# Warm-up products in fp32, and two loads moved behind DMA transposes, in a fused recurrent attention and MLP kernel

## The chip, the cores and the metric

The kernel runs on one core of one Trainium2 chip. The metric is the time of one execution in microseconds on the device. Before the change it is 179.27 us, the median of three runs (178.81, 179.27, 180.53).

In the text, PE is the matrix engine and PEld its loading of weights, DVE the vector engine, ACT the scalar engine, POOL the GpSimd engine, SP the engine that issues every DMA of this kernel. PSUM is the memory that PE writes to.

## What is computed

A linear recurrence with decay (4 sequences, 8 heads, 768 positions, head size 48) feeds a two-layer MLP with squared ReLU (width 384, inner width 2048). Cut to what matters:

```python
for t in range(S):                       # S = 768
    cur = einsum('bhd,bhe->bhde', u * k[t], v[t])
    y[t] = einsum('bhd,bhde->bhe', r[t], state + cur)
    state = w[t][..., None] * state + einsum('bhd,bhe->bhde', k[t], v[t])
x = y.transpose(0, 2, 1, 3).reshape(B * S, H * D)      # 3072 x 384
h = maximum(x @ w_in, 0)                               # 3072 x 2048
out = (h * h) @ w_out                                  # 3072 x 384
```

All inputs and the output are fp32 in HBM.

## The kernel before

The work is cut into 12 steps, each of 256 positions of one sequence (three steps to a sequence); two positions that follow each other share a partition. A step has an attention part and an MLP part, and the MLP of a step runs long after its attention, so that the attention of later steps fills in beside it.

**Attention of step s.** Loads bring r, k, v and w into fp32 tiles (four buffers for each, `load_step`, L179). `ww_`, `rw_` and `kw_` multiply the decays into the pairs of positions, `lw_` takes the logarithm, `cum_` sums the logarithms with triangular matrices on PE (L332 to L336), `exp_` turns the sums into decays (L348), `rd_` multiplies them into r and k (`rdec_buf` L366, `kdec_buf` L369). Both must be transposed. In the first steps PE does that (`tr_`, L382, then a copy out of PSUM, `rkt_`, L396); from step 4 on a DMA transpose does (`dtr_`, L401 for r, L404 for k). Then come the products r k (`p_`, L422 or L425), their mask on DVE (`pm_`, L438 or L441), the state (`su_`, `ts_`, `sn_`), the output (`y_`, L490, and `yc_`, L502), and the diagonal part with u (`ku_`, `qp_`, `q_`, `qs_`, `vq_`), which is added at the end in `ysb_` (L513). `ub_` (L212) spreads u over the partitions at the start with one fp32 product, and `uc_` copies it out of PSUM.

**MLP of step s.** x is transposed, by PE in the first steps (`yt_`, `xt_`), by DMA from step 6 on (`dyt_`, L534). `m1_` (L545) makes one eighth of the inner width, six products of 256 columns each; `rl_` and `sq_` are the squared ReLU; `m2_` (L576) adds four products of 384 columns into an output bank; `os_` scales it and `store` writes it out.

**What sets the order.** The order of all work is written out by hand, as one list of words (`ORDER`). A word such as `m1_.7.4:3` names an operation, its step and part, and after the colon the PSUM bank; `=A`, `=V` or `=G` names ACT, DVE or POOL. Each engine takes its own words strictly in the order of the list, and waits on the others by semaphores; all DMAs, the transposes among them, are issued by SP one after the other, and SP stops at a word whose input or buffer isn't ready. Where two words sit on different engines, their order in the list does not matter beyond that.

**Dummies.** `warm_.n.i.x` (L594) issues n products of a zero tile into bank i (banks 4 and 5 are the attention's, L596 is the line of each product). They compute nothing that is used: they keep PE busy in the first 24 us while it waits for loads and for DVE. The tile `warm` is cleared on DVE first (L234). There are 55 in all, in thirteen words: 11 before the sums of step 0; 8, 3 and 5 around its transposes; 3, 2 and 7 in one row ahead of the transposes of step 1; then 2, 2, 6, 4, 1 and 1.

The lists of SP around the two moved loads are, before the change: `store.4.1`, `ld.9.v`, `ld.10.k`, `dyt_.7`, `ld.10.v`, `store.4.0`, `dtr_.9.0`, `ld.10.r`, `dyt_.8`, `ld.11.w`, `dtr_.9.1`, `ld.11.v`.

Of the kernel before, what the change touches and what calls it, by code (L numbers as in the profile page):

```python
# [8 lines left out]
FP32 = mybir.dt.float32  # L9
FP16 = mybir.dt.float16  # L10
BF16 = mybir.dt.bfloat16
# [3 lines left out]


ORDER = """
ld.0.w ld.0.u ld.0.k ld.0.r ld.1.w ww_.0=V lw_.0 warm_.11.5.0 cum_.0:0 ub_.0:2 kw_.0=G exp_.0 uc_.0=A rd_.0.1 ld.0.v
warm_.8.5.1 tr_.0.1:0 rkt_.0.1=A ld.1.k ld.1.r rw_.0=G ld.2.w ku_.0=G rd_.0.0 ld.1.v warm_.3.5.2 tr_.0.0:1 ww_.1=V
rkt_.0.0=A qp_.0=V ld.2.r v_.0=A warm_.5.5.3 p_.0.0:m p_.0.1:1 ac_.0 lw_.1 q_.0 su_.0:b ld.2.k cum_.1:0 ts_.0.0=A  # L20
kw_.1=G pm_.0.0 pm_.0.1 vs_.0.0=A sn_.0.0 ld.1.i exp_.1 rw_.1=G vs_.0.1=A qs_.0=A warm_.3.2.4 ku_.1=G rd_.1.0 rd_.1.1
warm_.2.2.5 ts_.0.1=V qp_.1=V warm_.7.2.6 ld.0.i tr_.1.0:0 rkt_.1.0=V warm_.2.3.21 tr_.1.1:2 ac_.1 sn_.0.1 q_.1
# [40 lines left out]
p_.8.0:m p_.8.1:0 kw_.9=G qp_.9=G ysb_.7=V cum_.9:1 m2_.6.0.1:1 ld.9.v ld.10.k os_.5.0=A m2_.6.0.3 m2_.6.1.3:0  # L63
m2_.6.0.0 sq_.6.2=V m2_.6.0.2 m2_.6.1.0 sn_.8.0 al_.9 exp_.9 pm_.8.0 rd_.9.0 pm_.8.1 dyt_.7 v_.9=A ac_.9 m1_.7.7:2
y_.8:0 yc_.8.1 rd_.9.1 su_.9:1 vs_.9.1=A yc_.8.0 rl_.7.7=A m1_.7.4:3 ld.10.v vq_.8=G ysb_.8=V m1_.7.0:2 lw_.10
store.4.0 q_.9 rl_.7.4=A ts_.9.0=A rl_.7.0=A cum_.10:0 al_.10 vs_.9.0=V exp_.10 m2_.6.1.1 os_.6.0=V m2_.6.1.2
os_.6.1=A m1_.7.5:2 m1_.7.6:3 m1_.7.2:0 kw_.10=G dtr_.9.0 qs_.9=G rl_.7.5=A ld.10.r dyt_.8 ld.11.w sq_.7.2=A m1_.7.3:2
m1_.7.1:1 rl_.7.6=A dtr_.9.1 m1_.8.5:3 rl_.7.3=A rl_.7.1=A m1_.8.6:2 v_.10=G sn_.9.0 ts_.9.1=V rw_.10=G rd_.10.1
# [24 lines left out]
def kernel(  # L93
# [13 lines left out]
    nc = tc.nc  # L107
# [3 lines left out]
    C = 128  # L111
# [24 lines left out]
    consts = ctx.enter_context(tc.tile_pool(name="consts", bufs=1))  # L136
# [10 lines left out]
    att = [ps_att.tile([C, 2, 512], FP32, name=f"att{i}") for i in range(2)]  # L147
# [4 lines left out]
    quad = bk + m1_bank  # L152
# [63 lines left out]

    warm = consts.tile([C, 512], BF16)
    tri_strict = consts.tile([C, C], BF16)  # L220
    tri_incl_neg = consts.tile([C, C], BF16)
    ident = consts.tile([C, C], BF16)
# [369 lines left out]
        nc.sync.dma_start(out=out[t0:t0 + C, cols], in_=tiles["o", s, rows][:, cols])  # L592

    def warm_(n, i, x=0):  # L594
        for _ in range(n):
            nc.tensor.matmul(quad[i][:] if i < 4 else att[i - 4][:, 0, :], warm[:, 0:C], warm[:],  # L596
                             start=True, stop=True)

    def ld(n, x, h=None):
# [48 lines left out]
```

## Time and profile before

| | us |
|---|---|
| median of three runs | 179.27 |
| the profiled execution | 180.34 |
| its span, first to last instruction | 178.6 |
| PE busy | 172.8 (97%) |
| DVE busy | 138.9 (78%) |
| ACT busy | 134.0 (75%) |
| POOL busy | 109.7 (61%) |

The profile is of one execution. Times in it count from the first instruction. A row of a timeline is the start, the time until the last of the row's instructions ends, the engine, the line of the kernel, the operation, what it writes and reads, the shape, how many instructions the row holds, and in brackets the idle time of the engine before it with what ended it. The ends of PE's products are modelled and products are pipelined, so a row's end overlaps the next row's start. A product of PE appears as a matmul and a weight load (PEld). A few matmuls are missing from the records (51 of the 55 dummies are there). A row of SP shows when a DMA was issued, not when it landed; the median time from issue to landing stands in a table of the page.

### The profile page before, as it was taken

To read this page: it belongs to the slowest core of one execution; us is meant where nothing else is said; L and a number is where in the kernel's file an instruction comes from. 1 tells how busy PE (TensorE), PEld (TensorE's weight loads), DVE (VectorE), ACT (ScalarE), POOL (GpSimd) and SP (SyncE) were. 2 spreads that over 40 slices of the span, in tenths; PEclk is the share of its full clock that TensorE was granted. 3 is DMA by queue.
4 is the path that set the end of the run, shared out by engine and by line. 5 is a ranking of instruction groups with operands and counts; after the bars stand their busy time and mean duration, and the time that the engine had idled before them with its cause. 6 is when DMAs were issued, how large, how long until landed. Compare 5 with 4: busy or idle time off the path is not lost.

```text
span 178.6 us, 5531 instructions
## 1 busy us (share of the span) xinstructions
PE 172.8 (97%) x2296; PEld 125.6 (70%) x2300; DVE 138.9 (78%) x205; ACT 134.0 (75%) x240; POOL 109.7 (61%) x132
## 2 busy tenths in 40 slices
PE   7999999999999999999999999899999999999993
PEld 2365588887766777678677776588676778868763
DVE  5399999779999997998988999876678693803530
ACT  5478999999799759899789979579876528853601
POOL 6458999861765437997599689959997803000000
DMA  5999999999999499999999999998997650512212
GB/s 143 264 261 265 296 349 342 359 341 257 257 263 293 95 160 260 206 218 282 253 294 135 232 205 219 184 205 175 279 122 142 84 48 0 134 45 88 88 48 88
DMA packets 78954, 35.61 MB, mean 199 GB/s; under 512 B 72145, under 2 KB 77394, under 8 KB 78930
## 3 DMA queue, kind: packets, MB, share of 16 engines
q1 hardware_dynamic: 78930, 35.27, 89.9%
q8 instruction: 18, 0.29, 0.7%
q14 instruction: 6, 0.05, 0.1%
HBM read 25.17 MB, written 4.72 MB: 167 GB/s over the span
## 4 chain that ended last, share of the span: by engine, by line
PE 62%; POOL 15%; DVE 10%; DMA 6%; issue 5%; ACT 1%; POOLq 0%; SPq 0%; DVEq 0%; ACTq 0%
PE m L576 16%; PE bk L545 12%; PE m L545 11%; PE bk L576 10%; DMA k_raw<-in_k_dram 3%; PE att L596 3%; DVE pmT L441 3%; DMA kT<-kdec_buf 2%; POOL ku L305 2%; POOL ku L310 2%; PE att L490 2%; POOL qs L285 2%; POOL r_raw L294 2%; POOL ku L324 2%; POOL S L468 1%
## 5 line engine op out<-in xcount | busy, mean ns | idle before, releaser
L545 PEld LDWEIGHTS <-wi_sb 128*128 128x128 bf16 x576 | 54.9, 98 | 10.6 <-DMA xT<-y_sb 0.9
L576 PEld LDWEIGHTS <-gt 128*128 128x128 bf16 x400 | 37.7, 98 | 19.8
L545 PE MATMUL m<-xT,wi_sb 128*128 128x256 bf16 x306 | 40.2, 273 | 0.6 <-DMA xT<-y_sb 0.5
L562 ACT ACTIVATE gt<-gt 128x1024 bf16<-128x1024 f16 x37 | 38.1, 1051 | 0.5
L576 PE MATMUL bk<-wo_sb,gt 128*128 128x384 bf16 (+2 forms) x208 | 35.8, 314 | 0.0
L545 PE MATMUL bk<-xT,wi_sb 128*128 128x256 bf16 x270 | 35.7, 273 | 0.0
L576 PE MATMUL m<-wo_sb,gt 128*128 128x384 bf16 x192 | 35.0, 326 | 0.0
L554 ACT ACTIVATE gt<-m 128x512 f16<-128x512 f32 x33 | 19.4, 594 | 12.6 <-PE m L545 12.5
L554 ACT ACTIVATE gt<-bk 128x512 f16<-128x512 f32 x35 | 20.6, 596 | 7.5 <-PE bk L545 7.2
L556 DVE TENSOR_SCALAR gt<-m 128x512 f16<-128x512 f32 x18 | 12.3, 688 | 13.4 <-PE m L545 12.4
L441 DVE TENSOR_TENSOR pmT<-att,mask 128x1024 bf16<-128x1024 f32 x16 | 19.1, 1214 | 2.1 <-PE att L425 2.0
L324 POOL TENSOR_TENSOR ku<-v_sh,qs 128x768 f32<-128x768 bf16 x9 | 13.3, 1476 | 10.6 <-ACT qs L285 10.5
L468 POOL TENSOR_TENSOR S<-t_state,ac_buf 128x192 bf16<-128x192 f32 x20 | 11.7, 584 | 9.6 <-DVE t_state L463 7.0
L305 POOL TENSOR_TENSOR ku<-k_raw,u_bc 128x768 f32<-128x768 f32 x9 | 17.0, 1890 | 0.4 <-DMA k_raw<-in_k_dram 0.4
L513 DVE TENSOR_TENSOR y_sb<-att,ku 128x768 bf16<-128x768 f32 x12 | 11.4, 954 | 4.5 <-POOL k_raw L298 1.7
L298 POOL TENSOR_TENSOR k_raw<-k_raw,w_raw 128x384 f32<-128x384 f32 x8 | 8.4, 1048 | 10.0 <-DMA k_raw<-in_k_dram 10.0
L369 DVE TENSOR_TENSOR kdec_buf<-k_raw,att 128x768 bf16<-128x768 f32 x12 | 11.4, 947 | 3.7 <-ACT att L348 3.7
L285 ACT CAST v_sh<-v_raw 64x384 bf16<-64x384 f32 x26 | 13.2, 508 | 0.3
L310 POOL TENSOR_TENSOR ku<-ku,r_raw 128x768 f32<-128x768 f32 x7 | 12.7, 1810 | 0.2
L366 DVE TENSOR_TENSOR rdec_buf<-r_raw,att 128x384 bf16<-128x384 f32 x24 | 12.2, 545 | 0.4 <-POOL r_raw L294 0.4
L285 POOL CAST v_sh<-v_raw 64x384 bf16<-64x384 f32 x18 | 10.8, 598 | 1.3 <-DMA v_raw<-in_v_dram 0.6
L315 DVE TENSOR_REDUCE q<-ku 128x16 f32<-128x768 f32 x12 | 11.3, 942 | 0.0
(107 smaller groups left out, 257.0 us busy)
## 6 DMA issues: line engine op xcount, KB each, us to landing
w_raw<-in_w_dram SPq DMA_DIRECT2D x12, 384.0 KB, 5.9
k_raw<-in_k_dram SPq DMA_DIRECT2D x12, 384.0 KB, 6.3
r_raw<-in_r_dram SPq DMA_DIRECT2D x12, 384.0 KB, 5.7
v_raw<-in_v_dram SPq DMA_DIRECT2D x12, 384.0 KB, 6.0
out_dram<-o_sb SPq DMA_DIRECT2D x23, 192.0 KB, 4.5
w_st<-in_moe_w_in_dram SPq DMA_DIRECT2D x4, 768.0 KB, 10.3
w_st<-in_moe_w_out_dram SPq DMA_DIRECT2D x4, 768.0 KB, 9.0
kT<-kdec_buf SPq DMA_TRANSPOSE x8, 3.9
```

The costliest lines, as they stand in the source:

```text
L285: copy(out[j * Q:(j + 1) * Q, c], src[c * Q:(c + 1) * Q, :, j])
L305: tensor_mul("ku_", s, h)(tiles["ku", s][:, hs], raw["k", s][:, hs, 1:3, :], u_bc[:, hs, None, :].to_broadcast([C, n, 2, D]))
L310: tensor_mul("qp_", s, h)(ku, ku, raw["r", s][:, heads(h), 0:2, :])
L324: tensor_mul("vq_", s)(vq[:], tiles["vs", s][:], tiles["qs", s][:, :, :, None].to_broadcast([C, 2, H, D]))
L366: nc.vector.tensor_mul(rdec[0][:, ps, j, :, 0:D], x[:, :, j, :].rearrange("p (a e) d -> p a e d", e=2), dec.rearrange("p (a e) d -> p a e ...
L441: nc.vector.tensor_mul(pmT, ps_p[:].rearrange("p e (x t) -> p (e x) t", t=C), mk.to_broadcast([C, 8, C]))
L468: nc.gpsimd.tensor_mul(t[:], tiles.pop(("ts", s, c))[:].rearrange("p (a d) -> p a d", a=HP), tiles["a_c", s][:, :, c, None].to_broadcast([ ...
L545: nc.tensor.matmul(ps1[:, j, :], wi_sb[:, n // 4, kk, n % 4 * 128:(n % 4 + 1) * 128], tiles["xT", s][:, :, kk, :], start=(kk == 0), stop=( ...
L554: nc.scalar.activation(rl, m1, AF.Relu, scale=RS)
L556: nc.vector.tensor_scalar(out=rl, in0=m1, scalar1=RS, scalar2=0.0, op0=ALU.mult, op1=ALU.max)
L562: nc.scalar.activation(gt, rl, AF.Square)
L576: nc.tensor.matmul(m2, gt[:, 4 * q + n, rows * C:(rows + 1) * C], wo_sb[:, 4 * q + n, cols], start=(summed[s, c] == 1 and n == 0), stop=(s ...
```

## The change

The list of the change has three parts.

1. The dummies become fp32 products. The tile `warm` is fp32 instead of bf16. A word with n dummies now issues products of up to 512 columns, each of which stands for four of the old: 128 columns for each old dummy of 512, so n old dummies become n/4 products, rounded up, the last one narrower.
2. The word with eight dummies becomes one with four and stands some words earlier in the list. On PE its place is the same: behind `ub_`, ahead of `tr_.0.1`.
3. On SP, the k load of step 10 moves from ahead of `dyt_.7` to right behind it. The k transpose of step 9 (`dtr_.9.1`) moves ahead of the r load of step 10, `dyt_.8` and `ld.11.w`, so that it stands right behind `dtr_.9.0`. SP's list is then: `ld.9.v`, `dyt_.7`, `ld.10.k`, `ld.10.v`, `store.4.0`, `dtr_.9.0`, `dtr_.9.1`, `ld.10.r`, `dyt_.8`, `ld.11.w`, `ld.11.v`.

```diff
-... uc_.0=A rd_.0.1 ld.0.v
-warm_.8.5.1 tr_.0.1:0 ...
+... uc_.0=A warm_.4.5.1
+rd_.0.1 ld.0.v tr_.0.1:0 ...
...
-... m2_.6.0.1:1 ld.9.v ld.10.k os_.5.0=A ... pm_.8.1 dyt_.7 v_.9=A ...
+... m2_.6.0.1:1 ld.9.v os_.5.0=A ... pm_.8.1 dyt_.7 ld.10.k v_.9=A ...
...
-... dtr_.9.0 qs_.9=G rl_.7.5=A ld.10.r dyt_.8 ld.11.w sq_.7.2=A m1_.7.3:2
-m1_.7.1:1 rl_.7.6=A dtr_.9.1 m1_.8.5:3 ...
+... dtr_.9.0 qs_.9=G rl_.7.5=A dtr_.9.1 ld.10.r dyt_.8 ld.11.w sq_.7.2=A
+m1_.7.3:2 m1_.7.1:1 rl_.7.6=A m1_.8.5:3 ...
...
-    warm = consts.tile([C, 512], BF16)
+    warm = consts.tile([C, 512], FP32)
...
     def warm_(n, i, x=0):
-        for _ in range(n):
-            nc.tensor.matmul(quad[i][:] if i < 4 else att[i - 4][:, 0, :], warm[:, 0:C], warm[:],
-                             start=True, stop=True)
+        bank = quad[i][:] if i < 4 else att[i - 4][:, 0, :]
+        while n > 0:
+            m = 128 * min(n, 4)
+            nc.tensor.matmul(bank[:, 0:m], warm[:, 0:C], warm[:, 0:m], start=True, stop=True)
+            n -= 4
```

More of the change, by code (lines that the diff above doesn't have):

```diff
@@ L17 @@
 ORDER = """
-ld.0.w ld.0.u ld.0.k ld.0.r ld.1.w ww_.0=V lw_.0 warm_.11.5.0 cum_.0:0 ub_.0:2 kw_.0=G exp_.0 uc_.0=A rd_.0.1 ld.0.v
-warm_.8.5.1 tr_.0.1:0 rkt_.0.1=A ld.1.k ld.1.r rw_.0=G ld.2.w ku_.0=G rd_.0.0 ld.1.v warm_.3.5.2 tr_.0.0:1 ww_.1=V
+ld.0.w ld.0.u ld.0.k ld.0.r ld.1.w ww_.0=V lw_.0 warm_.11.5.0 cum_.0:0 ub_.0:2 kw_.0=G exp_.0 uc_.0=A warm_.4.5.1
+rd_.0.1 ld.0.v tr_.0.1:0 rkt_.0.1=A ld.1.k ld.1.r rw_.0=G ld.2.w ku_.0=G rd_.0.0 ld.1.v warm_.3.5.2 tr_.0.0:1 ww_.1=V
 rkt_.0.0=A qp_.0=V ld.2.r v_.0=A warm_.5.5.3 p_.0.0:m p_.0.1:1 ac_.0 lw_.1 q_.0 su_.0:b ld.2.k cum_.1:0 ts_.0.0=A
@@ L62 @@
 m2_.5.0.3 m2_.5.0.0 store.4.1 ku_.9=G q_.8 qs_.8=G ww_.10=G rl_.6.5=V vq_.7=V rl_.6.0=A vs_.8.1=A rw_.9=G sq_.6.0=A
-p_.8.0:m p_.8.1:0 kw_.9=G qp_.9=G ysb_.7=V cum_.9:1 m2_.6.0.1:1 ld.9.v ld.10.k os_.5.0=A m2_.6.0.3 m2_.6.1.3:0
-m2_.6.0.0 sq_.6.2=V m2_.6.0.2 m2_.6.1.0 sn_.8.0 al_.9 exp_.9 pm_.8.0 rd_.9.0 pm_.8.1 dyt_.7 v_.9=A ac_.9 m1_.7.7:2
+p_.8.0:m p_.8.1:0 kw_.9=G qp_.9=G ysb_.7=V cum_.9:1 m2_.6.0.1:1 ld.9.v os_.5.0=A m2_.6.0.3 m2_.6.1.3:0 m2_.6.0.0
+sq_.6.2=V m2_.6.0.2 m2_.6.1.0 sn_.8.0 al_.9 exp_.9 pm_.8.0 rd_.9.0 pm_.8.1 dyt_.7 ld.10.k v_.9=A ac_.9 m1_.7.7:2
 y_.8:0 yc_.8.1 rd_.9.1 su_.9:1 vs_.9.1=A yc_.8.0 rl_.7.7=A m1_.7.4:3 ld.10.v vq_.8=G ysb_.8=V m1_.7.0:2 lw_.10
 store.4.0 q_.9 rl_.7.4=A ts_.9.0=A rl_.7.0=A cum_.10:0 al_.10 vs_.9.0=V exp_.10 m2_.6.1.1 os_.6.0=V m2_.6.1.2
-os_.6.1=A m1_.7.5:2 m1_.7.6:3 m1_.7.2:0 kw_.10=G dtr_.9.0 qs_.9=G rl_.7.5=A ld.10.r dyt_.8 ld.11.w sq_.7.2=A m1_.7.3:2
-m1_.7.1:1 rl_.7.6=A dtr_.9.1 m1_.8.5:3 rl_.7.3=A rl_.7.1=A m1_.8.6:2 v_.10=G sn_.9.0 ts_.9.1=V rw_.10=G rd_.10.1
+os_.6.1=A m1_.7.5:2 m1_.7.6:3 m1_.7.2:0 kw_.10=G dtr_.9.0 qs_.9=G rl_.7.5=A dtr_.9.1 ld.10.r dyt_.8 ld.11.w sq_.7.2=A
+m1_.7.3:2 m1_.7.1:1 rl_.7.6=A m1_.8.5:3 rl_.7.3=A rl_.7.1=A m1_.8.6:2 v_.10=G sn_.9.0 ts_.9.1=V rw_.10=G rd_.10.1
 rd_.10.0 ac_.10 ku_.11=G rl_.7.2=A rl_.8.5=V sq_.7.1=A ld.11.v m1_.8.7:1 p_.9.0:1 p_.9.1:0 m1_.8.1:3 ww_.11=G
```

## The prediction

> **What bounds the kernel now.** I read the page first, then the busy time by stretches, then the timelines of the opening and of the middle, engine by engine.
>
> ```profile
> PE 172.8 (97%) x2296; PEld 125.6 (70%) x2300; DVE 138.9 (78%) x205; ACT 134.0 (75%) x240; POOL 109.7 (61%) x132
> ```
> ```profile
> 15.00:19.00 4.00, 3.84 (x51) 2.33 (x50) 4.00 (x8) 3.33 (x10) 3.44 (x4) 1.00 1.19 243
> 19.00:23.00 4.00, 3.81 (x65) 2.09 (x66) 4.00 (x6) 3.87 (x10) 4.00 (x5) 1.00 0.99 338
> 23.00:112.00 89.00, 88.75 (x1274) 67.43 (x1274) 82.00 (x117) 79.20 (x139) 65.61 (x72) 1.00 1.10 250
> 112.00:126.00 14.00, 13.05 (x207) 10.16 (x205) 9.69 (x16) 11.08 (x22) 11.45 (x15) 1.00 1.14 190
> ```
>
> The columns are the stretch, its length, then busy time of PE, PEld, DVE, ACT and POOL, the granted clock, the DMA share and GB/s. There are two regimes. Up to about 23 us DVE has no free moment (4.00 of 4.00, twice) and PE is padded with dummies. From 23 us on PE is the bound: 88.75 of 89.00. The only place after that where it visibly idles is 112 to 126, by 0.95 us. So the change can act in three ways only: it can move the moment when the PE-bound part begins, it can add to or take from PE's own work, and it can take away that 0.95.
>
> **The opening, part by part.**
>
> ```profile
> 1.19 4.87 PE L596 MATMUL att<-warm 128*128 128x512 bf16 x11 [1.19 <-DVE warm L234]
> ...
> 6.28 0.53 PE L336 MATMUL att<-lw_buf,tri_incl_neg 128*128 128x384 bf16 x1
> 6.74 0.93 PE L212 MATMUL m<-u_row,ones_row 1*128 1x384 f32 x2
> 7.60 1.90 PE L596 MATMUL att<-warm 128*128 128x512 bf16 x8
> 9.34 0.61 PE L382 MATMUL bk<-ident,kdec_buf 128*128 128x128 bf16 x8
> ...
> 13.81 2.75 PE L596 MATMUL m<-warm 128*128 128x512 bf16 x11
> ```
>
> Eight dummies fill 7.60 to 9.34, 0.217 us each; the first eleven need 0.43 each (4.87 less a pipelined tail of some 0.18, by 11), although the granted clock of every stretch reads 1.00. So PE is slow at first and at full speed by 7.60.
>
> The trace has one fp32 product, the one that spreads u: one product of 384 columns is two records, and it holds PE from 6.74 to 7.60, 0.86 us. At the dummies' later rate (0.217 for 512 columns) 384 bf16 columns take 0.163, so this one costs 5.3 times a bf16 product of its width. The new dummies need four times exactly to be free, since a fourth as many columns are issued for each old dummy. The lower end is that four: the row before (6.28 to 6.74, 0.46 us for 384 bf16 columns) shows that PE was still slow just then, and a product with one row of weights between products of 128 rows may pay for the change of shape. The upper end is 5.3, a third more than before. I take 4.1, nearer to the low end, because the slow row stands directly before it.
>
> ```profile
> 6.86 0.19 PEld L212 LDWEIGHTS m<-u_row,ones_row 1*128 1x128 f32 x1
> ```
> ```profile
> L596 PEld LDWEIGHTS <-warm 128*128 128x128 bf16 x55 | 5.4, 106 | 7.7 <-issue 3.0 <-DVE warm L234 1.2
> ```
>
> A rule of the Trainium skill speaks against the change: by "TensorE: Matmul & The Clock Gate", section "Weight-path perf modes", the fast weight load is not used for fp32 inputs. Where the trace agrees: the fp32 load took 0.19 us, and the bf16 loads of the dummies 0.11 in the mean. Taken alone the rule would add some 0.1 us for each load that nothing hides. The first row above shows the second load at 6.86 while the product issued at 6.74 is running, so I count loads as hidden wherever a record streams longer than a load.
>
> **The first eleven** become three products of 512, 512 and 384 columns: the same column time. Their tile is twice as wide in bytes, so the memset that they wait for is longer.
>
> ```profile
> 0.86 0.27 DVE L234 MEMSET warm<- 128x256 uint32 x1 [0.86 <-PEq L634]
> ...
> 7.73 0.95 DVE L369 TENSOR_TENSOR kdec_buf<-k_raw,att 128x768 bf16<-128x768 f32 x1 [2.71 <-ACT att L348]
> 8.60 1.01 DVE L366 TENSOR_TENSOR rdec_buf<-r_raw,att 128x384 bf16<-128x384 f32 x2
> 9.53 1.65 DVE L272 TENSOR_TENSOR ww<-w_raw 128x384 f32<-128x384 f32 x1
> ```
> ```profile
> 8.94 1.83 POOL L305 TENSOR_TENSOR ku<-k_raw,u_bc 128x768 f32<-128x768 f32 x1
> ```
>
> At most one more memset of 0.27 goes ahead of the first dummy, so the sums of step 0, its exponential and DVE's start at 7.73 move by up to 0.27, by 0.4 with some fp32 excess. I cost this at nothing, and the cover is the squared weights of step 1 at 9.53: they take 1.65 us and end at 11.18, 0.41 after POOL's product (8.94 + 1.83 = 10.77), so they seem to wait for POOL, and POOL's product hangs on loads that do not move. A start 0.4 later still ends near 11.2. Without that cover the whole kernel would be 0.3 to 0.4 later. The four dummies left out save 0.87 of PE before the transposes at 9.34. That gains nothing by itself: their input is ready at 8.68 (7.73 + 0.95) or later, and what comes after is DVE's row of work without a gap.
>
> **The later dummies** (3+2+7, 2, 2, 6, 4, 1, 1: 28 old dummies, 6.1 us) stand where PE has little room: 0.16 us idle in 15 to 19 and 0.19 in 19 to 23. At 4.1 times they add 6.1 x 0.1/4 = 0.15, at four times nothing, at 5.3 times 2.0 us. After the room of 0.35 that is 0 to 1.65 us by which the PE-bound part begins later; DVE's own work does not get longer. I take +0.1, as the two single dummies become records so short that their loads show.
>
> **The middle.**
>
> ```profile
> 115.08 0.83 PE L545 MATMUL m<-xT,wi_sb 128*128 128x256 bf16 x6 [0.55 <-DMA xT<-y_sb]
> ...
> 125.55 0.65 PE L425 MATMUL att<-rT,kT 64*64 64x128 bf16 x32 [0.40 <-DMA kT<-kdec_buf]
> ```
> ```profile
> 107.11 0.53 SPq L179 DMA_DIRECT2D k_raw<-in_k_dram  x1
> 109.97 1.22 SPq L534 DMA_TRANSPOSE xT<-y_sb  x1
> ...
> 114.94 0.57 SPq L179 DMA_DIRECT2D r_raw<-in_r_dram  x1
> 118.05 1.22 SPq L534 DMA_TRANSPOSE xT<-y_sb  x1
> ...
> 121.11 1.83 SPq L404 DMA_TRANSPOSE kT<-kdec_buf  x1
> ```
> ```profile
> DMA to landing us min/median/max: 2.7/3.1/5.1
> ```
>
> These are the 0.95: PE waits 0.55 for x of step 7 and 0.40 for k transposed of step 9. Both waits are what the change touches. The first transpose is issued at 109.97 and its reader starts at 115.08, 5.1 later, the slowest of six where the median is 3.1. The k load of step 10 was issued 2.9 us before it and is in its way; behind it, the transpose should land near 113.1 (109.97 + 3.1), 1.4 us ahead of when PE comes. The second is issued at 121.11 only because the r load, the next x transpose and a w load stand ahead of it on SP.
>
> ```profile
> 114.46 0.94 DVE L369 TENSOR_TENSOR kdec_buf<-k_raw,att 128x768 bf16<-128x768 f32 x1
> ```
>
> Its input is written at 115.40 (114.46 + 0.94), so in its new place it is issued about 115.45, 5.7 us sooner. Even with the slowest landing it is there when PE asks, from 125.0 on. So 0.95 goes; since a PE row's end holds the tail of some 0.16 (1.90 against 9.34 - 7.60), up to 0.16 more at each: 0.95 to 1.27. I take 1.1.
>
> What the moves delay: the k load is issued near 111.3 instead of 107.1, the r load near 117.1 instead of 114.9. The x transpose of step 8 is ready for SP at the same time as before but now has a transpose and the r load right ahead of it.
>
> ```profile
> 116.01 1.01 POOL L298 TENSOR_TENSOR k_raw<-k_raw,w_raw 128x384 f32<-128x384 f32 x1
> ...
> 121.34 1.01 POOL L294 TENSOR_TENSOR r_raw<-r_raw,w_raw 128x384 f32<-128x384 f32 x1
> ```
> ```profile
> k_raw<-in_k_dram SPq DMA_DIRECT2D x12, 384.0 KB, 6.3
> r_raw<-in_r_dram SPq DMA_DIRECT2D x12, 384.0 KB, 5.7
> ```
>
> By the medians k lands at 117.6 and r at 122.8: 1.6 and 1.5 us after POOL reads them now. Behind POOL's k product stand the diagonal sums of step 9, behind its r product the u product of step 11 and then the diagonal of step 9. PE is not fed by these within 2 us, so I cost them at nothing; if the cover is gone, up to 1.5 us.
>
> **Sum.** -1.1 + 0.1 = -1.0 us. The profiled execution took 180.34 (a span of 178.6 and 1.74 around it), so it would take 179.3; it lay 1.07 above the median of 179.27, so the median goes to 178.3.
>
> **Rivals.**
>
> *PE becomes the bound of the opening* (chance 0.21). If fp32 columns cost more than four times, each later dummy group pushes the sums, transposes and copies behind it. Price at the upper end +1.65; with the gain of 1.1 the kernel ends 0.55 slower, 179.8; where the waits also stay, 180.9. It outweighs the gain above (1.1 + 0.35)/6.1 = 24% excess. For it: 0.86 us measured. Against it: the slow clock there.
>
> *The wait moves on* (0.2). The x transpose of step 8 now lies behind two more transfers. Its reader is three groups of six products ahead of 125.55, about 123.0, and 122.3 once the first wait is gone; it lands at 121.2 by the median, at 123.2 at the slowest. It would give back up to 0.9, so the kernel ends near 179.0.
>
> *The pauses are not of the loads' making* (0.12).
>
> ```profile
> 112.00:114.00 2.00, 2.00 (x14) 1.21 (x13) 2.00 (x4) 1.41 (x4) 2.00 (x2) 1.00 1.51 91
> ```
> ```profile
> q8 instruction: 18, 0.29, 0.7%
> ```
>
> While the transpose of step 7 was under way the DMA engines were at their busiest (1.51) and moved only 91 GB/s. If something else than the load stops the transfers, the transpose lands as late as before or the next one does: no gain, 179.3. By the Trainium skill, "Runtime: NRT & Kernel Launch", section "Instruction fetch mechanics", instructions come in blocks of 16 KiB, 256 each. That fits the row (18 packets, 0.29 MB) and PE's 4596 records; with some 38 fewer records ahead, every later fetch would fall at another moment, for better or worse.
>
> *The clock comes up later with fewer, longer products* (0.04): PE at half speed for a few us more, 0 to 3 us, 180.5.
>
> **How the numbers follow.** The forecast has 0.43 (its own range 177.6 to 178.8, from the bounds 0.95 to 1.27 and 0 to 0.35); the rivals hold the rest. The range 177.2 to 180.3 takes in the forecast, the moved wait, the pauses and most of the first rival, and the spread of the runs (178.81 to 180.53) at both ends. One per cent, 1.8 us, is what a measurement of this kernel can tell from no change: below 177.5 needs the whole gain and a lucky median, 0.12; above 181.1 needs the upper end of the first rival with the waits unchanged, or the clock, 0.1; within, 0.78.
>
> **What would show it.** Right: the dummies of 13.81 take 2.6 us as 8 fp32 records; the first m2 or attention work after 23 us starts within 0.2 of now; no PE idle on x of step 7 or k transposed of step 9; the latter issued near 115.5. Wrong: an fp32 record of 512 columns spaced well over 0.43 us; PE idle on x of step 8; POOL idle on r of step 10 with DVE and PE behind it.

## The result and the profile after

The changed kernel takes 181.36 us in the median of five runs (181.20 to 182.26), the kernel before 179.69 in five runs beside them. The ratio on record is 1.0083 with a 95% interval of 1.0055 to 1.0112 (the two medians alone would give 1.0093): slower by 0.8%, where 0.6% faster was forecast. 181.36 lies above the range given (177.2 to 180.3).

The profiled execution of the changed kernel took 181.36 us too, with a span of 179.6. The one profiled before the change took 180.34, which is 0.65 above the median of its five runs. So the kernel before was profiled once more (label e0_before below: 179.55 us, span 177.8, at the median). The comparisons here are made against that second profile.

First a line of the page of the changed kernel, then its busy time by stretches (columns as in the prediction), then the last two of these stretches of the kernel before, second profile.

```profile
PE 173.2 (96%) x2281; PEld 126.9 (71%) x2281; DVE 140.7 (78%) x205; ACT 134.1 (75%) x240; POOL 110.3 (61%) x132
```
```profile
15.00:19.00 4.00, 4.00 (x49) 2.82 (x48) 4.00 (x8) 2.69 (x8) 3.30 (x4) 1.00 1.19 250
19.00:23.00 4.00, 4.00 (x63) 2.17 (x61) 4.00 (x6) 3.84 (x11) 4.00 (x5) 1.00 1.00 352
23.00:112.00 89.00, 88.92 (x1281) 67.80 (x1279) 82.13 (x118) 79.45 (x139) 66.62 (x72) 1.00 1.06 247
112.00:126.00 14.00, 13.12 (x208) 10.27 (x207) 9.97 (x17) 10.69 (x21) 10.00 (x13) 1.00 1.09 222
126.00:145.00 19.00, 18.39 (x332) 13.26 (x331) 15.49 (x21) 12.52 (x20) 16.09 (x21) 1.00 0.67 120
```
```profile
112.00:126.00 14.00, 13.51 (x212) 10.79 (x211) 10.28 (x17) 11.40 (x22) 12.17 (x15) 1.00 1.03 197
126.00:145.00 19.00, 19.00 (x341) 13.86 (x339) 15.27 (x25) 11.69 (x18) 14.12 (x20) 1.00 0.72 131
```

Up to 112 us nothing visible was lost: 88.92 busy of 89.00. Between 112 and 126 PE idles 0.88 us (14.00 less 13.12) where the kernel before idles 0.49. And there is a new loss from 126 to 145, 0.61 us, where the kernel before has none.

The same rows of PE in both kernels show where the time goes. Timeline of PE, kernel before (second profile):

```profile
115.97 1.48 PE L545 MATMUL m<-xT,wi_sb 128*128 128x256 bf16 x12
...
122.13 1.47 PE L545 MATMUL m<-xT,wi_sb 128*128 128x256 bf16 x12
...
124.75 0.65 PE L425 MATMUL att<-rT,kT 64*64 64x128 bf16 x32 [0.49 <-DMA kT<-kdec_buf]
...
136.66 0.82 PE L576 MATMUL m<-wo_sb,gt 128*128 128x384 bf16 x4
...
142.09 0.46 PE L425 MATMUL att<-rT,kT 64*64 64x128 bf16 x16
```

Timeline of PE, changed kernel:

```profile
116.01 1.48 PE L545 MATMUL m<-xT,wi_sb 128*128 128x256 bf16 x12
...
123.21 1.48 PE L545 MATMUL m<-xT,wi_sb 128*128 128x256 bf16 x12 [0.88 <-DMA xT<-y_sb]
...
125.28 0.65 PE L425 MATMUL att<-rT,kT 64*64 64x128 bf16 x32
...
138.36 0.82 PE L576 MATMUL m<-wo_sb,gt 128*128 128x384 bf16 x4 [0.32 <-ACT gt L562]
...
143.94 0.43 PE L425 MATMUL att<-rT,kT 64*64 64x128 bf16 x16
```

At 116 us the two kernels are level (115.97 and 116.01). Then the changed one loses 1.04 on x of step 8 (123.21 against 122.13, less the 0.04), wins back 0.55 because k transposed of step 9 is there (125.28 against 124.75), loses 1.17 more by the row at 138.36, and stands 1.85 behind at 143.94. The spans differ by 1.8. So the whole loss of this pair of executions arises in 28 us in the middle, in three places. (The changed kernel had begun its PE-bound part 0.47 later, at 25.82 against 25.35. The kernel before loses 0.43 of that near 85 us, where its PE pauses and the changed kernel's does not.) (The loss is more than the idle time of the stretches, since the modelled ends of PE's rows cover part of each pause.)

**The first place: x of step 8.** SP's own timeline, changed kernel:

```profile
114.90 1.57 SPq L401 DMA_TRANSPOSE rT<-rdec_buf  x1
116.56 1.49 SPq L404 DMA_TRANSPOSE kT<-kdec_buf  x1
118.10 0.57 SPq L179 DMA_DIRECT2D r_raw<-in_r_dram  x1
118.77 1.25 SPq L534 DMA_TRANSPOSE xT<-y_sb  x1
```
```profile
116.21 0.96 DVE L513 TENSOR_TENSOR y_sb<-att,ku 128x768 bf16<-128x768 f32 x1 [0.94 <-POOL ku L324]
```

The input of the x transpose is written at 117.17 (DVE's row, 116.21 + 0.96). SP is then busy with the k transpose (till 118.05) and the r load, and issues it at 118.77, 1.6 later.

**The second place: POOL, and through it DVE.** Rows of POOL and of DVE, changed kernel:

```profile
122.51 1.00 POOL L294 TENSOR_TENSOR r_raw<-r_raw,w_raw 128x384 f32<-128x384 f32 x1 [1.98 <-DMA r_raw<-in_r_dram]
...
130.40 1.82 POOL L305 TENSOR_TENSOR ku<-k_raw,u_bc 128x768 f32<-128x768 f32 x1
```
```profile
130.74 1.89 DVE L294 TENSOR_TENSOR r_raw<-r_raw,w_raw 128x384 f32<-128x384 f32 x1
```

The same, kernel before (second profile):

```profile
120.45 1.00 POOL L294 TENSOR_TENSOR r_raw<-r_raw,w_raw 128x384 f32<-128x384 f32 x1
...
127.85 2.14 POOL L305 TENSOR_TENSOR ku<-k_raw,u_bc 128x768 f32<-128x768 f32 x1
```
```profile
127.52 0.79 DVE L298 TENSOR_TENSOR k_raw<-k_raw,w_raw 128x384 f32<-128x384 f32 x1
...
130.01 0.55 DVE L294 TENSOR_TENSOR r_raw<-r_raw,w_raw 128x384 f32<-128x384 f32 x1
```

POOL waits 1.98 for r of step 10 and is 2.06 late afterwards (122.51 against 120.45). Because of that its u product of step 10 (L305) stands at 130.40 to 132.22 instead of 127.85 to 129.99, and covers the moment when DVE comes to r of step 11 (L294). DVE's product takes 1.89 us instead of 0.55 and ends at 132.63, 0.41 after POOL's. Before, DVE's k product (L298) got in 0.33 us ahead of POOL's, and L294 came 0.02 after POOL's end. Behind L294 on DVE stand the sums, and behind them the exponential and the decays of step 11, on which the work of PE around 137 depends.

**The third place** is what PE then lacks: 0.32 on `gt` at 138.36 and smaller pauses ahead of it (0.12 at 133.29, 0.16 at 136.87).

### The profile page after: what moved, and what is told of

It reads as the page before. It is cut to its first block, busy times and chain, and to the rows that moved or that the text cites. A ratio compares the mean times of both kernels' runs of the same rounds, so it can differ in the third digit from the quotient of the medians.

```text
span 179.6 us, 5499 instructions
## 1 busy us (share of the span) xinstructions
PE 173.2 (96%) x2281; PEld 126.9 (71%) x2281; DVE 140.7 (78%) x205; ACT 134.1 (75%) x240; POOL 110.3 (61%) x132
## 4 chain that ended last, share of the span: by engine, by line
PE 53%; POOL 15%; DMA 14%; DVE 6%; issue 4%; SPq 4%; ACT 2%; POOLq 0%; DVEq 0%; ACTq 0%
PE m L576 11%; PE bk L545 10%; PE m L545 10%; PE bk L576 8%; DMA out_dram<-o_sb 6%; DMA k_raw<-in_k_dram 6%; SPq L179 4%; POOL ku L305 3%; DMA xT<-y_sb 2%; PE m L598 2%; POOL ku L310 2%; POOL ww L272 2%; PE bk L598 2%; PE att L490 2%; POOL ku L324 2%
## 5 line engine op out<-in xcount | busy, mean ns | idle before, releaser
L305 POOL TENSOR_TENSOR ku<-k_raw,u_bc 128x768 f32<-128x768 f32 x9 | 16.7, 1853 | 1.0 <-DMA k_raw<-in_k_dram 1.0
L298 POOL TENSOR_TENSOR k_raw<-k_raw,w_raw 128x384 f32<-128x384 f32 x8 | 8.6, 1069 | 10.9 <-DMA k_raw<-in_k_dram 10.9
L310 POOL TENSOR_TENSOR ku<-ku,r_raw 128x768 f32<-128x768 f32 x7 | 12.7, 1811 | 0.2
L285 POOL CAST v_sh<-v_raw 64x384 bf16<-64x384 f32 x18 | 12.1, 670 | 1.0 <-DMA v_raw<-in_v_dram 0.2
L348 ACT ACTIVATE att<-att 128x768 f32<-128x768 f32 x12 | 9.6, 800 | 2.9 <-DVE att L341 1.7
```

Source lines behind the costliest of these rows:

```text
L285: copy(out[j * Q:(j + 1) * Q, c], src[c * Q:(c + 1) * Q, :, j])
L305: tensor_mul("ku_", s, h)(tiles["ku", s][:, hs], raw["k", s][:, hs, 1:3, :], u_bc[:, hs, None, :].to_broadcast([C, n, 2, D]))
L310: tensor_mul("qp_", s, h)(ku, ku, raw["r", s][:, heads(h), 0:2, :])
```

## The experiments

All ratios are against the kernel before, run in turn on the same chip. Medians of the kernel before in the five batches: 179.58, 179.53 (two batches), 179.34 and 179.26.

### The kernel before, once more

No edit.

> The kernel before, a second profile of it. The first profile belongs to an execution of 180.34 us, 0.8 above the median of 35 runs (179.58). If that execution was an ordinary one, PE waits again for x of step 7 (0.55) and k transposed of step 9 (0.40), and the span is about 178.6 for a time of 180.3. If it was an unlucky one, at least one of these waits is shorter or gone and the span is near 177.8.

179.55 us, span 177.8. PE's row on x of step 7 starts at 114.20 and has no wait; only the wait for k transposed of step 9 is there (0.49, quoted above). So one of the two waits which the prediction wanted to remove comes and goes between executions, and the gain to be had here was about half of what the first profile showed. Thirteen of the profiles are of kernels that leave the k load of step 10 in its old place; the wait for x of step 7 stands in three of them (0.55 in the first profile, 0.47 in e6_more, 0.53 in e14_kt_one_up). In the seven with the k load moved it stands in none.

### The two halves of the change

The opening alone (e1_opening): the dummies as changed, SP's list as before.

> The opening of the changed kernel (fp32 dummies, four fewer) with the middle as it was before. Theory (the loss is made by the k transpose of step 9 in its new place, which pushes the r load of step 10 and the x transpose of step 8 back): the PE-bound part begins 0.2 us later, as in the changed kernel (25.82 against 25.63), the waits of the middle stay, and the time is that of before plus 0.2 to 0.4 us, ratio 1.001 to 1.002. Rival (the dummies do the harm, by moving the moments at which instructions are fetched against the DMA transposes): the time is that of the changed kernel, ratio 1.006 to 1.011, with new waits of PE on transposes in the middle.

180.60 us, ratio 1.0063 (1.0042 to 1.0083): the rival's ratio. Both moves with the old dummies (e2_moves):

> Both moves on SP with the opening of before. Theory: PE waits about 1 us for x of step 8 and loses another 1 us between 132 and 139, as in the changed kernel; ratio 1.004 to 1.009. Rival (dummies): no such wait, both waits of before gone, ratio 0.994 to 0.997.

180.34 us, 1.0048 (1.0028 to 1.0068): the theory's ratio, with PE waiting 1.26 for x of step 8. The k load alone (e3_k_load):

```diff
-... m2_.6.0.1:1 ld.9.v ld.10.k os_.5.0=A ... pm_.8.1 dyt_.7 v_.9=A ...
+... m2_.6.0.1:1 ld.9.v os_.5.0=A ... pm_.8.1 dyt_.7 ld.10.k v_.9=A ...
```

> Only the k load of step 10 moved behind the x transpose of step 7. Theory: the wait for x of step 7 (0.55 by its row, 0.71 by the spacing of the products) is gone, the wait for k transposed of step 9 stays, nothing new comes; ratio 0.995 to 0.998. Rival (the transpose was held up by an instruction fetch, not by the load): the transpose still lands 4 us or more after its issue, PE still waits, ratio 1.000.

179.93 us, 1.0015 (0.9991 to 1.0040): not the theory's gain, although PE has no wait for x of step 7 here (its transpose lands 3.6 us after its issue) and 0.17 for k transposed. What is new is a wait of POOL's for the r load, 0.96. The k transpose alone (e4_k_transpose):

```diff
-... rl_.7.5=A ld.10.r dyt_.8 ld.11.w ... rl_.7.6=A dtr_.9.1 ...
+... rl_.7.5=A dtr_.9.1 ld.10.r dyt_.8 ld.11.w ... rl_.7.6=A ...
```

> Only the k transpose of step 9 moved ahead of the r load of step 10, the x transpose of step 8 and the w load. Theory: this part alone makes the loss: the wait for k transposed (0.40) goes, but PE waits for x of step 8 (0.3 to 1.0) and DVE and ACT come late between 131 and 139 (about 1 us); POOL waits 1 to 2 us for r of step 10; ratio 1.003 to 1.010. Rival (dummies): ratio 0.997 to 1.000.

180.17 us, 1.0037 (1.0012 to 1.0061): the theory's ratio, with 1.24 of POOL's waiting for r of step 10, but only 0.14 of PE's for x of step 8. So both halves cost: 1.1 us and 0.9 us by the ratios, 2.0 together, where the whole costs 1.5 with an interval that reaches 2.0. Whether they add up stays open. Of the moves, the k load can't be told from nothing, and the k transpose alone costs 0.7.

The opening alone loses its time far from the opening. Timeline of PE and rows of DVE and POOL, opening alone:

```profile
125.04 0.65 PE L425 MATMUL att<-rT,kT 64*64 64x128 bf16 x32 [0.72 <-DMA kT<-kdec_buf]
...
137.51 0.82 PE L576 MATMUL m<-wo_sb,gt 128*128 128x384 bf16 x4 [0.32 <-ACT gt L562]
...
143.09 0.43 PE L425 MATMUL att<-rT,kT 64*64 64x128 bf16 x16
```
```profile
127.81 1.77 DVE L298 TENSOR_TENSOR k_raw<-k_raw,w_raw 128x384 f32<-128x384 f32 x1
...
130.63 1.16 DVE L294 TENSOR_TENSOR r_raw<-r_raw,w_raw 128x384 f32<-128x384 f32 x1
```
```profile
123.24 1.02 POOL L272 TENSOR_TENSOR ww<-w_raw 128x384 f32<-128x384 f32 x1
...
127.35 1.82 POOL L305 TENSOR_TENSOR ku<-k_raw,u_bc 128x768 f32<-128x768 f32 x1
```

The first of these rows of POOL in the kernel before (second profile):

```profile
123.75 1.00 POOL L272 TENSOR_TENSOR ww<-w_raw 128x384 f32<-128x384 f32 x1 [0.51 <-DMA w_raw<-in_w_dram]
```

Against the second profile of before it is 0.29 behind at k transposed of step 9, 0.85 at the row of 136.66, and 1.00 at that of 142.09. Here POOL is not late. DVE is 0.29 late (127.81 against 127.52), since its mask of step 9 waits for PE, which waits for k transposed; and POOL is 0.50 early (127.35 against 127.85), since it need not wait for the w load. So POOL's L305 is now 0.46 ahead of DVE's L298 instead of 0.33 behind, and L298 takes 1.77.

### The number of instructions ahead of the middle

In the profile an fp32 product is two matmuls and two weight loads. The 18 such products hold 72 instructions where the 55 dummies held 110, 38 fewer. (The page counts 4596 before and 4562 after, with some records missing.) Padding puts tiny products (two columns, into a bank that the attention overwrites; their results are not used) behind the second dummy word (`warm_.4.5.1`) to make up for these 38 (e5_pad):

```diff
+    def pad_(n, i):
+        for _ in range(n):
+            nc.tensor.matmul(att[i - 4][:, 0, 0:2], tri_strict[:], half_ones[:], start=True, stop=True)
...
-... warm_.4.5.1 rd_.0.1 ...
+... warm_.4.5.1 pad_.19.5 rd_.0.1 ...
```

> The opening of the changed kernel, the middle of before, and 19 products of two columns where the four dummies were left out: PE then has as many instructions as before. Theory (the opening costs 1.1 us because 38 fewer instructions of PE move every later instruction fetch against the DMA transposes): ratio 1.000 to 1.003, the opening's own 0.2 us. Rival (the fp32 products themselves cost it, through the later start or the clock): ratio 1.005 to 1.008 as without the 19.

179.48 us, 0.9990 (0.9967 to 1.0014). The whole loss of the opening is gone, with the fp32 dummies still in place. The same direction with old dummies, two of them replaced by 21 tiny products, so 38 instructions more than before (e6_more):

> The kernel before with bf16 dummies, six for eight in the second word, and 21 products of two columns behind them: 38 more instructions of PE, hardly more time in the opening. Theory (fetch moments decide): the time moves, by up to 1 us to either side, with the PE-bound part beginning within 0.2 us of before. Rival (the fp32 products): ratio 0.999 to 1.002.

179.23 us, 0.9981 (0.9958 to 1.0005): no difference, so the shift that the theory allowed did not come. Old dummies with 19 of them left out, 38 instructions fewer than before (e7_fewer):

> The kernel before with 19 of its 55 bf16 dummies left out (3 of 11, all 8, 4 of 7, 2 of 6, 2 of 4): as many PE instructions as in the changed kernel, without any fp32. Theory (fetch moments decide): ratio 1.004 to 1.008, as the changed opening alone. Rival (the fp32 products): ratio 0.998 to 1.001, unless PE idles so long that its clock falls, which would show as products at twice their time.

181.67 us, 1.0105 (1.0075 to 1.0135). Its own opening runs out of cover (PE is busy 3.51 of 4.00 in 15 to 19, and 1.08 behind the second profile of before at 24 us), so only the rest, some 1.0 us that it loses between 121 and 142, speaks for the theory. PE's wait for k transposed of step 9 is 1.04 in it.

The padding at the other end (e12_late_pad): 19 tiny products behind the last product of the kernel, so that the program is as long as before but the middle comes 38 instructions earlier in it.

```diff
-... m2_.11.3.0 m2_.11.3.3 store.11.1 ...
+... m2_.11.3.0 m2_.11.3.3 pad_.19.5 store.11.1 ...
```

> The opening change alone, with the 19 two-column products not in the opening but behind the last product of the kernel, where PE has nothing left to do. The number of PE instructions in the whole program is as before, the number ahead of the stretch from 110 to 140 us is 38 lower. Theory (the place of the instructions counts: what comes ahead of 110 us decides which transfers the fetches of instructions fall on): as with the opening change alone, 1.004 to 1.008, with DVE's products L298 or L294 of step 11 over 1 us in the profile. Rival (the length of the whole program counts, by the layout of code or by the number of blocks): 0.997 to 1.001, as with the padding in the opening. At the end itself the products cost nothing, since the last stores outlast them (at most 0.5 us).

180.75 us, 1.0069 (1.0041 to 1.0098), the same as the opening alone, with L298 at 1.45 and L294 at 1.15. So it is the place of the middle in PE's stream that acts and not the length of the program. Half the padding (10 tiny products in place of 19, e13_half_pad):

> The opening change alone with 10 two-column products in the opening in place of 19: 18 PE instructions fewer than before instead of 38. Theory (where the fetches fall decides, and that is met or missed): it lies anywhere from 0.998 to 1.007, and the time goes with the duration of DVE's L298 and L294 of step 11: under 1.000 if both are below 0.8 us, above 1.003 if either is above 1.1. Rival (the padding fills a gap of the opening itself, for each product a little): half way, 1.002 to 1.004, with L294 and L298 not deciding.

179.51 us, 1.0001 (0.9976 to 1.0025): not half of the loss but none of it, with L298 at 0.88 and L294 at 0.55. (The profiled execution, 178.73, is 0.8 below the median; PE waits for neither x of step 7 nor k transposed in it.) The effect goes by hit or miss. 18 instructions fewer than before cost nothing and 38 fewer cost 1.1 us.

What the place decides can be seen in part in the transfers. Two rows of the DMA tables, opening alone: the queue of instructions in 122 to 124 us (packets, megabytes, share of the engines), and the k transpose of step 9 (last figure: us from issue to landing):

```profile
q8 instruction: 1, 0.02, 3.4%
```
```profile
kT<-kdec_buf SPq DMA_TRANSPOSE x1, 5.9
```

The same with the padding, where the block comes in 117 to 119 and none in 122 to 124:

```profile
q8 instruction: 1, 0.02, 5.1%
```
```profile
kT<-kdec_buf SPq DMA_TRANSPOSE x1, 4.4
```

In the opening alone a block of PE's instructions is fetched while the k transpose is under way, and that lands 5.9 us after its issue; with the padding it lands after 4.4. It is also issued 0.93 sooner in the opening alone (119.11 against 120.04), so it lands only some 0.6 later. The w load of step 11, which POOL's L272 reads, goes the other way: with the padding the block comes while this load is under way, and it lands 5.2 after its issue; in the opening alone it lands after 4.0.

The other kernels agree. Five have the k transpose of step 9 in its old place and 38 instructions fewer ahead of it (e1, e7, e8, e12, e16). All five fetch a block in 122 to 124 us; the transpose lands after 5.9 to 6.2 and the w load after 4.0 to 4.3. In the six other profiles with the transpose in its old place (both of before, e3, e5, e6, e13), no block comes there; the transpose lands after 4.4 to 5.4 and the w load after 4.5 to 5.2. But in e13_half_pad, which loses nothing, a block comes beside the transpose too, in 119 to 121, and it lands after 5.2. So a block beside it is not enough; its moment counts.

It is inferred, not shown, that the fetch is what slows the transpose: the fetch could not be moved by itself, and other transfers (the w load, a v load, an r load and stores) share the engines at that time. The prediction named the rule on this, from the Trainium skill, "Runtime: NRT & Kernel Launch", section "Instruction fetch mechanics". That blocks hold 256 instructions and 16 KiB fits; that the crossing is mostly hidden does not fit this kernel, if the inference holds: 38 instructions decide over 1.1 us (1.0063 against 0.9990).

### Whole change with the padding

The changed kernel with `pad_.19.5` as above (e11_after_pad):

> The changed kernel with 19 products of two columns where the four dummies were left out, so that PE has as many instructions as before. Theory (the opening costs through the number of PE instructions): what is left is the cost of the two moves alone, ratio 1.003 to 1.007 (1.0048 measured with the bf16 dummies). Rival (the cost is not in the number): ratio 1.0083.

180.59 us, 1.0059 (1.0032 to 1.0085): between the change (1.0083) and the moves alone (1.0048), and told apart from neither. It is still slower than before, so the padding doesn't mend the moves.

### What the k transpose delays

It is moved only past the w load of step 11; r load and x transpose stay (e14_kt_one_up):

```diff
-... dyt_.8 ld.11.w ... rl_.7.6=A dtr_.9.1 ...
+... dyt_.8 dtr_.9.1 ld.11.w ... rl_.7.6=A ...
```

> The kernel before with k transposed of step 9 moved up only past the w load of step 11, behind the x transpose of step 8; the r load and the x transpose stay where they were. Theory (the move of the change costs because it delays the r load and x of step 8, not because the transpose is early): PE no longer waits for k transposed (0.3 to 0.6 us), nothing new appears, 0.996 to 1.000. Rival (what the transpose no longer waits for is found again further on, as the whole attention chain of step 11 sets the pace from 125 to 140): 0.999 to 1.003, the wait gone from the profile and 0.3 to 0.6 us more idle of PE between 132 and 145.

180.76 us, 1.0075 (1.0047 to 1.0103). Neither expected ratio came; if anything the kernel is slower than with the move past three words (1.0037). POOL and DVE, this kernel:

```profile
125.63 1.00 POOL L272 TENSOR_TENSOR ww<-w_raw 128x384 f32<-128x384 f32 x1 [1.94 <-DMA w_raw<-in_w_dram]
...
129.94 1.81 POOL L305 TENSOR_TENSOR ku<-k_raw,u_bc 128x768 f32<-128x768 f32 x1
```
```profile
130.29 1.88 DVE L294 TENSOR_TENSOR r_raw<-r_raw,w_raw 128x384 f32<-128x384 f32 x1
```

k transposed is there in time, and POOL waits 1.94 for the w load, which the transpose pushed back. From there on it is the picture of the changed kernel: L305 late, L294 covered, ending 0.42 after it. So it isn't the r load or x of step 8 as such. In both kernels the load that stands right behind the k transpose on SP's list comes late for POOL: r there, w here. The profile of this execution also has a wait for x of step 7 (0.53), which the edit does not touch.

### Taking DVE's product out of the way

DVE's r product of step 11 behind the sums of step 11, with the opening alone (e8_open_rw) and with the whole change (e9_after_rw):

```diff
-... ts_.10.0=V rw_.11=V ... al_.11 exp_.11 ...
+... ts_.10.0=V ... al_.11 rw_.11=V exp_.11 ...
```

> The changed opening with the middle of before, and DVE's r product of step 11 placed behind the sums of step 11 (al) instead of ahead of them. Theory (the lost time of the changed opening comes from two fp32 products of DVE, k and r of step 11, that now start while POOL holds a product of its own, 1.77 and 1.16 us instead of 0.78 and 0.55, and hold up the exponential of step 11): the r product falls into DVE's idle time ahead of the decayed k, the sums end 0.5 to 1 us earlier, PE's wait near 137.5 (0.53) goes; ratio 1.001 to 1.004 instead of 1.0063. Rival (the transposes alone make the loss): ratio 1.005 to 1.008 as before, with PE still waiting at 137.

180.49 us, 1.0056 (1.0030 to 1.0082): the rival's ratio. But DVE's product was not out of POOL's way here. L294 takes 1.87 in its new place, behind POOL's L310, and L298 takes 1.67, so this run does not decide between the two.

> The changed kernel with the same one product moved. Theory: the r product (1.89 us in the changed kernel, 0.55 in a second profile of before) no longer stands ahead of the sums; PE's waits between 132 and 139 (1.1 us over the usual) go, the wait for x of step 8 (1.0) stays; ratio 1.000 to 1.004 instead of 1.0083. Rival (the wait for x of step 8 alone makes the loss): no gain, ratio 1.007 to 1.010.

180.77 us, 1.0065 (1.0043 to 1.0087), between the two expectations, with L294 at 0.78. PE does not wait for x of step 8 in this execution, but 0.80 for r of step 8 at 110 us. With the old dummies, the k load behind `dyt_.7`, the k transpose behind `dyt_.8` and the same move of `rw_.11` (e10_mix):

> The opening of before; the k load of step 10 behind the x transpose of step 7; the k transpose of step 9 right behind the x transpose of step 8, ahead of the w load only; the r product of step 11 behind the sums. Theory: no wait for x of step 7 or 8, the wait for k transposed (0.56 in the second profile of before) gone, no collision ahead of the sums: 0.5 to 0.8 us faster than before, ratio 0.995 to 0.998. Rival (PE's waits are replaced by others as fast as they go): ratio 0.999 to 1.003.

180.05 us, 1.0016 (0.9997 to 1.0035): the rival's ratio, although every wait that the theory named is gone. In e9 and e10 the pauses of PE between 132 and 139 are gone and others stand at 142 and 143, on the state and on `y_sb` (0.34 and 0.40 in both, by the spacing of PE's products across the pause, which is 0.04 without one). In e8 the wait for k transposed (0.82) stays, and one for r of step 8 (0.85) stands at 110 us, which the opening alone does not have.

### Taking POOL's product out of the way

On POOL the u product of step 10 goes behind three short casts; the work is the same (e15_after_swap with the whole change, e16_open_swap with the opening alone, e17_kt_swap with the old dummies and the k transpose one place up).

```diff
-... ku_.10=G ... vs_.11.1=G v_.11=G ac_.11 ...
+... vs_.11.1=G v_.11=G ku_.10=G ac_.11 ...
```

> The changed kernel with one word moved on POOL alone: the u product of step 10 (one product of 1.8 us that reads SBUF) goes behind the casts of v of step 11 (three casts of 0.5 to 0.8 us); POOL's total work is the same. Theory (DVE's r product of step 11 cannot end before the POOL instruction that was running when it started, plus 0.4 us; with 1.8 us of POOL in front of it the chain of step 11, logarithm sums, exponential and k decay, is late): L294 falls from 1.89 to 1.0 or less, PE's idle between 132 and 139 falls by 0.5 us or more, ratio 1.001 to 1.006. Rival (POOL's lateness itself, by the r load that comes late, sets the end, wherever the two meet): L294 falls but the time stays at 1.007 to 1.010, with the idle found at 140 to 144 on the diagonal part.

181.22 us, 1.0091 (1.0058 to 1.0123): the rival was right. L294 took 0.68 and the pauses from 132 to 139 fell, but the kernel is as slow as the change. (The profiled execution is its fastest, 1.0 below the median.)

> The opening change alone with the same move on POOL. Theory: L298 and L294 of step 11 (1.77 and 1.16 us with the opening change alone) fall to 1.0 or less each, ratio 0.999 to 1.003; the wait for k transposed of step 9 (0.9 us) stays and costs what is left. Rival (that wait, and not the meeting of DVE and POOL, makes the 1.1 us): 1.005 to 1.007.

180.15 us, 1.0053 (1.0030 to 1.0075), with L298 at 0.55 and L294 at 0.98. The rival again: the wait for k transposed (1.04) stays.

> The kernel before with k transposed of step 9 one place up (ahead of the w load) and the same move on POOL. Theory: the w load comes late on POOL as in the run without the move (1.9 us idle), but DVE's L294 meets a short cast instead of the 1.8 us product: L294 falls from 1.88 to 1.0 or less, ratio 0.998 to 1.003 where it was 1.0075. Rival (POOL 1.9 us late is late for the diagonal part too): 1.004 to 1.008, with PE or DVE waiting for POOL at 139 to 144.

179.86 us, 1.0028 (0.9999 to 1.0058), against 1.0075 without the move on POOL. Here the ratio is the theory's, and the waits that the rival named are there too. PE in this kernel, then POOL in this kernel and in the second profile of before:

```profile
142.07 0.31 PE L502 MATMUL att<-S,rT 64*64 64x48 bf16 x16 [0.16 <-POOL S L468]
...
142.59 0.43 PE L425 MATMUL att<-rT,kT 64*64 64x128 bf16 x16 [0.21 <-DVE y_sb L513]
```
```profile
141.50 0.51 POOL L468 TENSOR_TENSOR S<-t_state,ac_buf 128x192 bf16<-128x192 f32 x1
```
```profile
140.90 0.51 POOL L468 TENSOR_TENSOR S<-t_state,ac_buf 128x192 bf16<-128x192 f32 x1
```

In the kernel before, POOL's state is written at 141.41. PE's row that reads it runs from 141.79, and its second half comes to about 141.94, so POOL is some half a microsecond ahead. With the w load 1 us late on POOL (L272 at 124.82 against 123.75) the state is written at 142.01, and PE waits. These two waits (0.35 and 0.40 us by the same spacing) are the same as in e9, e10 and e15. So the meeting of DVE and POOL is one way in which a late load costs, about 0.8 us of it here (1.0075 against 1.0028, with intervals that overlap a little), and the lateness of POOL alone is another, which takes its place when the first is removed.

No version beat the kernel before.

## Why the prediction was wrong

**The opening's own terms held.** Rows of PE, of DVE and of POOL, changed kernel:

```profile
6.33 0.32 PE L334 MATMUL att<-lw_buf,tri_strict 128*128 128x384 bf16 x1
6.49 0.32 PE L336 MATMUL att<-lw_buf,tri_incl_neg 128*128 128x384 bf16 x1
6.75 0.91 PE L212 MATMUL m<-u_row,ones_row 1*128 1x384 f32 x2
7.58 1.13 PE L598 MATMUL att<-warm 128*128 128x512 f32 x2
...
13.85 2.85 PE L598 MATMUL m<-warm 128*128 128x384 f32 x8 [0.39 <-DVE pmT L438]
16.54 0.61 PE L382 MATMUL bk<-ident,rdec_buf 128*128 128x128 bf16 x8
...
25.82 0.82 PE L545 MATMUL bk<-xT,wi_sb 128*128 128x256 bf16 x6
```
```profile
9.66 1.68 DVE L272 TENSOR_TENSOR ww<-w_raw 128x384 f32<-128x384 f32 x1
```
```profile
9.11 1.81 POOL L305 TENSOR_TENSOR ku<-k_raw,u_bc 128x768 f32<-128x768 f32 x1
```

The twelve dummies from 13.85 are 8 fp32 records, and the next work starts 2.69 later (2.6 forecast). Twelve old dummies of 0.217 are 2.60, so an fp32 column costs 4 x 2.69/2.60 = 4.1 times a bf16 one, as taken. The reason given for 4.1 did not hold, and that the number came out is in part luck. The prediction put the 5.3 of the product that spreads u down to a PE that was still slow in the row before. Here PE is at full speed there (384 bf16 columns from 6.33 to 6.49, 0.16), and the u product still holds it from 6.75 to 7.58, 0.83, or 5.1 times; in the second profile of before it is 0.84. What makes that one product dearer than the dummies stays open. The memset took 0.48 instead of 0.27 and is hidden where the prediction said: the squared weights end at 11.34, 0.42 after POOL's product (9.11 + 1.81 = 10.92), so POOL sets their end. That product starts between 8.54 and 9.15 in the profiles, with either kind of dummy. (The words of three and of five dummies had no term in the sum. They take 0.70 and 1.26 here, 9.23 to 9.93 and 10.38 to 11.64, against 0.65 and 1.26 before, under the same cover.) The PE-bound part begins at 25.82 in the changed kernel; it began at 25.63 and 25.35 in the two profiles of before, and at 25.25 and 25.38 with fp32 dummies in e13_half_pad and e12_late_pad. That is the spread of executions and not the price of fp32.

**The rival that PE becomes the bound of the opening** (0.21, 179.8) did not happen: PE, as busy as can be there, ended on time. The room of 0.35 that it counted on is not there in the second profile of before, where PE is busy 4.00 of 4.00 in both stretches. Nor did the clock come later: in the changed kernel PE is at full speed from 6.33 on, by the row above. (The granted clock can't show it: it reads 1.00 in every stretch, also where the first dummies run at half speed.)

**Two steps failed. The first is that the moves delay loads and "I cost them at nothing".** The reason given, "PE is not fed by these within 2 us", looked only at the next 2 us of PE. POOL waited 1.98 for the r load and was 2.06 late, where the prediction had 1.5; POOL's lateness reached PE 10 to 20 us later, through DVE's product of step 11 and, in the runs with that product out of the way, through the state of step 10 and `y_sb` at 142. The prediction had named "up to 1.5 us" as the price if the cover is gone; the runs show 0.9 us for both moves. It had the mechanism in its hands: it read that the squared weights at 9.53 "seem to wait for POOL" because they ended 0.41 after its product. The same 0.41 stands at 132.63. It didn't ask where else DVE's fp32 products would meet POOL's if POOL moved by 1.5. Two of its own signs of being wrong were these: PE idle on x of step 8, and POOL idle on r of step 10 with DVE and PE behind it.

**The gain was over-read.** The 0.95 of idle came from an execution 0.65 above the median, and the wait for x of step 7 in it comes and goes. In the second profile only k transposed is waited for, 0.49. The two waits did go: x of step 7 and k transposed of step 9 have no idle in the changed kernel. The k transpose was issued at 116.56 and not at 115.45, since the store ahead of it and the r transpose took SP until then.

**The rival that the wait moves on** (0.2) was right in its place and size: PE waits 0.88 on x of step 8 where "up to 0.9" was given. In the other profiles with both moves the wait is 1.26, 0.77, 0.36 and nothing, so the size is that of one execution. It was one of three losses, and the sum had it as an alternative instead of a term.

**The second step that failed is the opening's sum, +0.1,** which had no term for 38 instructions fewer. The rival on the pauses (0.12) had named this cause and priced it wrongly. It said that 38 fewer records put every later fetch at another moment, "for better or worse", and priced that as no gain, 179.3. It was worse by 1.1 us, which the padding takes away. A price on both sides and a larger chance were missing. (It also read the stretch from 112 to 114 as the DMA engines' busiest, at 1.51. In the same profile 106 to 108 has 1.61 and 118 to 120 has 1.60.)

**The range** took in no case in which the middle loses more than it gains. (The forecast's own range, 177.6 to 178.8, is also wider than its bounds make it: 0.95 to 1.27 gained and 0 to 0.35 lost give 178.0 to 178.7.) "Slower" had 0.1, from the opening's upper end with the waits unchanged and from the clock; neither was what happened.

## What to carry to other kernels

Where one queue issues all transfers, moving one forward is moving each one behind it back: follow the late load through the engine that reads it until that engine has slack again, not for the next 2 us. Take a wait of half a microsecond as a thing to win only when a second profile shows it too. Before work is taken out of an engine's stream, or put in, count instructions as well as time; a padded copy of the kernel that keeps the count tells the two apart.

## What the runs showed of the hardware

**DVE and POOL shut each other out to the end of an instruction.** A DVE product of two fp32 tiles in SBUF (128x384) that starts while POOL runs an instruction ends 0.41 or 0.42 us after that one: in the changed kernel 132.63 against 132.22, with the k transpose one place up 132.17 against 131.75, with the opening alone 129.58 against 129.17. Alone it takes 0.55. In the twenty profiles 155 such products start while POOL runs an instruction; 112 end 0.41 to 0.42 after it, and the other 43, which start in its last 0.12 us, take their 0.55. Where DVE comes first, POOL's product of 1.82 takes 2.14. By the Trainium skill, "SBUF — State Buffer", section "Who interferes with whom", a DVE instruction with two inputs in SBUF contends with a GpSimd instruction that reads SBUF, and whichever issues first holds the shared ports to its end. The traces agree in all these rows.

**Order by a hair.** The kernel before has DVE's k product 0.33 us ahead of POOL's u product, and its r product 0.02 us behind the end of it. Either half of the change makes the same two engines meet: the opening by a DVE that is 0.29 late and a POOL that is 0.50 early, the moves by a late POOL. The meeting makes one product of 0.55 last up to 1.89. What that costs the kernel depends on what else is late: with POOL's product out of the way the kernel with the k transpose one place up came down from 1.0075 to 1.0028, but the whole change and the opening alone stayed at 1.0091 and 1.0053.

**18 instructions or 38.** 38 instructions fewer in the first 24 us cost 0.6% (with the opening alone, and with the padding at the end), 18 fewer cost nothing, and 38 more cost nothing. The time is lost some 90 us later, between 117 and 142 us. That the fetches of instructions carry it there, by delaying a transfer, fits the traces and is inferred.
